# Two blocks of the first projection split into a 4-pair and a 2-pair part, and a new written order of all engines' work

## The chip, the cores and the metric

The kernel runs on one core of a Trainium2 chip. The core has a matrix engine (TensorE, "PE" in the profile, with its weight loads as "PEld"), three engines for element-wise work (VectorE "DVE", ScalarE "ACT", GpSimd "POOL"), and a fifth queue, SyncE ("SP"), which here only issues DMAs. ScalarE and GpSimd issue some DMAs too. Each engine works through its own list in order; semaphores make it wait for the others. The metric is the device time of one execution in microseconds.

## The reference

Attention with normalised queries and keys, then a feed-forward layer. Inputs are `q`, `k`, `v` of 8 batches x 12 heads x 448 positions x 64, gains `g_q`, `g_k`, and the weights `w_in` (768 x 2048) and `w_out` (2048 x 768), all float32.

```python
def rmsnorm(x, g):
    rms = np.sqrt(np.mean(x * x, axis=-1, keepdims=True) + 1e-06)
    return x / rms * g
q_n, k_n = (rmsnorm(q, g_q), rmsnorm(k, g_k))
scores = scale * np.matmul(q_n, k_n.transpose(0, 1, 3, 2))
...
attn = attn / (np.sum(attn, axis=-1, keepdims=True) + 1e-09)
return np.matmul(attn, v).astype(np.float32)
```

The attention's output is laid out as 3584 tokens x 768, and then:

```python
h = x @ w_in
g = h * (1.0 / (1.0 + np.exp(-1.702 * h)))
return (g @ w_out).astype(np.float32)
```

## The kernel before

**Pairs, batches and halves.** Two heads make a pair: 48 pairs, numbered 0 to 47, six to a batch. A pair's 448 positions stand on 112 partitions as four slices. The pairs of batch 0 are worked in two halves of the query positions (half 0, half 1); all later pairs are worked whole. In this text a step is named by its letter and its numbers:

- L(i,w): load of q (w=0), k (1) or v (2) of pair i, 224 KB, a DMA of SP or ACT (`load`, L860).
- S(i): squares, on ACT or POOL (`square`, L869). R(i): their sums, on DVE (`reduce`, L878). In pairs 0 and 1 each of them is split in two.
- Q(i): one over the root. In batch 0 by a logarithm and an exponential on ACT (`by_log`, L892); later for three pairs at once, a seed Q0 on DVE and eight small instructions on POOL.
- N(i,g): q (g=0) or k (1) times that, as bf16, on POOL or DVE (`norm`, L926).
- T(i,g): transpose to 64 x positions, on TensorE for pairs 0 to 11 (four small matmuls), by DMA for later ones. KQ(i), K(i): copies of it out of PSUM, K with the gains; for later pairs KQ scales in place, on DVE or ACT.
- V(i): v as bf16, on DVE or POOL (`vcast`, L933).
- C(i,h,t): scores, on TensorE. E(i,h,t): their exponential, on ACT, 112 x 896 elements. Two PSUM tiles take turns, so a score waits for the exponential two before it.
- P(i,h,w,x): attention times values, on TensorE, into one PSUM tile. O(i,h,w): the division, on DVE, which frees that tile.
- B(i,h): transpose of the result, on TensorE for pairs 0 to 11. X(i,h): its copy into the columns of the first projection's input, `xt`, on DVE.
- F(b,m): a block of the first projection of batch b (`first`, L1221). For batch 0 a block is 12 matmuls of 128 x 224: two slices of the 2048 columns of `w_in`, by six pairs, for one half of the positions; blocks 0 to 7 are half 0. H(b,m): tanh on ACT. G(b,m): the gate on DVE, which frees the block's PSUM bank.
- Y(p,t,h,c): a quarter of a token tile of the second projection of batches 2p and 2p+1. From batch 1 on part of the second projection, and in the last two batches of the first too, is done with seven products in place of eight, with sums of operands made on DVE (TT, S1 to S4, WT, XT).
- WI(c): four DMAs of 768 KB that POOL issues, a quarter of `w_in` each (`load_in`, L1193). Blocks 0 and 1 read WI(0), blocks 2 and 3 WI(1), 4 and 5 WI(2), 6 and 7 WI(3). WO(c): the same for `w_out` (`load_out`, L1199); Y(0,t,0,c) read WO(0) and WO(1), Y(0,t,1,c) WO(2) and WO(3).

**What sets the order.** The order of every engine's list is written out by hand in the table `ORDER` (L206 on), which also says on which engine a step runs that can run on two. A planner in the class `_Order` (L33) walks through these lists when the program is built, with a cost for each step, and emits the instructions in the order of its own clock. This clock decides nothing on an engine's order. It decides three smaller things: which free PSUM bank or output buffer a step takes, how many fill matmuls stand in a planned gap of TensorE (`fill`, L825; they multiply by zeros and write an unused bank), and, in the first 70 us of its clock, a dependency that keeps some POOL instruction behind a DVE instruction which uses the port that both share (`after_lock`, L848). The planner's constants at the top of the file (L25 to L30) tell how DMAs share the bandwidth and how long they take to begin.

**DMA lanes.** The DMAs of SP and ACT take eight semaphores in turn, so the ninth is issued only when the first has landed. A load also waits until its buffer is free: there are seven buffers for rows while i is below 14, so L(7,w) waits for N(0,g), L(13,w) for N(6,g).

**PSUM banks.** Until block F(0,0) two banks serve T and B ("w"); from that block on there are three, and the blocks of the projections take them too. A block holds its bank from its first matmul to its gate.

**The order at the start.** TensorE's list has F(0,0) after C(4,1,1), F(0,1) after B(1,1), and then one block every few steps up to F(0,15); the second projection's Y(0,0,0,0) follows. F(0,0) needs X(0..5, half 0). ACT's list has the squares, the Q steps and the exponentials of batch 0; a table load stands just before E(3,1,1) and H(0,0).

Of the kernel before, what the change touches and what calls it, by code (L numbers as in the profile page):

```python
# [24 lines left out]
BOTH, WITH_SW, SW_WITH = 0.63, 0.52, 0.65  # L25
BEGIN = {"SP": 740.0, "ACT": 760.0, "POOL": 3600.0, "DVE": 1010.0, "PE": 1400.0, "none": 0.0}
LANES, LANDS, KNOWN = 8, 1850.0, 500.0
NEVER = 1e12
APART = 45000.0
# [3 lines left out]
class _Order:  # L33
# [36 lines left out]
    def run(self):  # L70
# [74 lines left out]
        while emitted < len(self.tasks):  # L145
# [40 lines left out]
            if t.moves:  # L186
                t.rest, t.there, t.end = t.moves, free[eng] + LANDS, NEVER
# [14 lines left out]
    def open(self, name, now):  # L202
# [5 lines left out]
        ('R', 0, 1), ('R', 0, 0), ('R', 1, 0), ('R', 1, 1), ('N', 0, 1), 'g', ('KQ', 0), 'gG',  # L208
        ('K', 0), ('R', 2, 0), ('R', 3, 0), ('KQ', 1), ('K', 1), ('N', 2, 0), ('O', 0, 0, 0),
        ('R', 4, 0), ('KQ', 2), ('K', 2), ('KQ', 3), ('V', 1), ('X', 0, 0), ('K', 3), ('V', 2),  # L210
        ('O', 1, 0, 0), ('KQ', 4), ('K', 4), ('R', 5, 0), ('O', 2, 0, 0), ('X', 1, 0), ('V', 5),
        ('O', 3, 0, 0), ('N', 5, 1), ('X', 2, 0), ('KQ', 5), ('K', 5), ('O', 4, 0, 0), ('X', 3,
        0), ('X', 4, 0), ('O', 0, 1, 0), ('R', 6, 0), ('O', 5, 0, 0), ('X', 5, 0), ('X', 0, 1),
        ('O', 1, 1, 0), ('R', 7, 0), ('R', 8, 0), ('Q0', 8), ('X', 1, 1), ('O', 2, 1, 0), ('G',
        0, 0), ('O', 3, 1, 0), ('X', 2, 1), ('G', 0, 1), ('R', 10, 0), ('X', 3, 1), ('O', 4, 1,
        0), ('G', 0, 2), ('KQ', 6), ('K', 6), ('G', 0, 3), ('X', 4, 1), ('O', 5, 1, 0), ('G', 0,
        4), ('R', 9, 0), ('G', 0, 5), ('KQ', 7), ('K', 7), ('G', 0, 6), ('KQ', 8), ('X', 5, 1),
        ('K', 8), ('R', 11, 0), ('Q0', 11), ('G', 0, 7), ('G', 0, 9), ('G', 0, 8), ('V', 6),
        ('N', 11, 1), ('G', 0, 10), ('N', 10, 0), ('N', 10, 1), ('N', 11, 0), ('O', 7, None, 0),
        ('G', 0, 12), ('G', 0, 11), ('G', 0, 13), ('O', 6, None, 0), ('N', 9, 1), ('N', 9, 0),  # L220
        ('G', 0, 14), ('R', 12, 0), ('G', 0, 15), ('R', 13, 0), ('KQ', 9), ('K', 9), ('O', 7,
        None, 1), ('R', 14, 0), ('O', 6, None, 1), ('Q0', 14), ('KQ', 11), ('V', 8), ('KQ', 10),
# [438 lines left out]
def kernel(  # L661
# [22 lines left out]
    HALF = DM // 2  # L684
    WIN = 128
    AW = (NS - 1) * SS + WIN
    ON_PE = NP * 2
    FILL, FILL_GAPS = 1.2, 0.6
    SINGLE = NP

# [131 lines left out]
    def bank():  # L822
        return banks[od.got]
# [977 lines left out]
```

## Time and profile before

| | us |
|---|---|
| median of 5 runs | 412.49 |
| lowest, highest | 412.06, 413.67 |
| the profiled execution, whole | 412.19 |
| its span | 410.4 |
| TensorE busy | 401.7 (98%) |
| VectorE busy | 307.7 (75%) |
| ScalarE busy | 300.9 (73%) |
| GpSimd busy | 179.8 (44%) |

The profile is of one execution. Its span runs from the first instruction to the last; 1.8 us of the execution's own time lie around it. A line of the order-of-time view has the start in us, the length in us, the engine, the source line, the operation, the tiles (out<-in), the shape and the count; what stands in brackets is the idle time of the engine just before and what ended it. A group that follows without a bracket came with no idle time before it. Matmuls are pipelined, so the length of a group of them is longer than the time after which the next can start; the spacing from start to start says what one costs. The granted clock is the share of full speed that TensorE was given: 0.996 on the mean here.

### The profile page before, as it was taken

The page shows a single profiled execution, that of the slowest core. Times are in us where ns is not written, and L with a number is a line of the kernel's source. Part 1 is how long each engine was busy: PE and PEld are TensorE (multiplying, and loading weights), DVE is VectorE, ACT ScalarE, POOL GpSimd, SP SyncE. Part 2 cuts the span into 40 slices and gives each one's busy share as a digit, 9 for nine tenths or more (in the row PEclk, how much of TensorE's full clock was granted, in tenths as well). Part 3 has the DMA queues.
Part 4 walks back from the last instruction along what each step waited for, and adds up shares of the span by engine and source line. Part 5 has one row for each costly group of instructions (what it writes and reads, how often), then busy time and mean ns, then how long its engine had stood idle before and what let it go on. Part 6 is the DMA issues. An engine that isn't in the chain of part 4 may idle for free.

```text
span 410.4 us, 9991 instructions
## 1 busy us (share of the span) xinstructions
PE 401.7 (98%) x3848; PEld 237.6 (58%) x3848; DVE 307.7 (75%) x628; ACT 300.9 (73%) x452; POOL 179.8 (44%) x272
## 2 busy tenths in 40 slices
PE   6999999999999999999999999999999999999996
PEld 5658876565555555565555555555555665555664
DVE  3879897789899977867786687878665889653742
ACT  4899887898887878887897767878888624584211
POOL 5787915974926194839614368346700200000000
PEclk9899999999999999999999999999999999999999
DMA  8999999969584797764875795954653124000065
GB/s 210 239 243 236 239 227 249 233 164 200 150 222 94 184 198 205 189 166 115 222 196 135 150 237 135 182 125 118 169 124 69 43 56 122 2 0 2 14 171 144
DMA packets 101776, 63.38 MB, mean 154 GB/s; under 512 B 55008, under 2 KB 101728, under 8 KB 101728
## 3 DMA queue, kind: packets, MB, share of 16 engines
q1 hardware_dynamic: 91840, 53.98, 54.9%
q0 software_dynamic: 7360, 6.29, 9.5%
q10 hardware_dynamic: 2528, 2.47, 2.5%
q8 instruction: 30, 0.49, 0.5%
q14 instruction: 18, 0.15, 0.1%
HBM read 45.61 MB, written 11.01 MB: 138 GB/s over the span
## 4 chain that ended last, share of the span: by engine, by line
PE 91%; DMA 2%; ACT 2%; POOL 1%; DVE 1%; issue 1%; DVEq 0%; ACTq 0%
PE w L1226 27%; PE w L1321 21%; PE o L1020 13%; PE sc L999 11%; PE b L1321 6%; PE b L1610 4%; PE w L1256 4%; PE w L1610 3%; DMA rows<-in_k_dram 2%; ACT sq L876 1%; ACT att L1009 1%; PE w L952 1%; POOL row L929 1%; PE w L1046 1%; POOL late L942 1%
## 5 line engine op out<-in xcount | busy, mean ns | idle before, releaser
L1007 ACT ACTIVATE att<-sc 112x896 bf16<-112x896 f32 x168 | 146.1, 917 | 26.7 <-PE sc L999 26.3
L1226 PE MATMUL w<-xt,w_in_s 128*128 128x448 bf16 (+1 forms) x672 | 120.9, 326 | 0.1
L1020 PEld LDWEIGHTS <-att 112*128 112x128 bf16 x1536 | 66.6, 98 | 35.7 <-issue 12.3
L1226 PEld LDWEIGHTS <-w_in_s 128*128 128x128 bf16 x672 | 60.5, 97 | 40.6 <-issue 6.5
L929 POOL TENSOR_TENSOR row<-rows,rs 112x512 bf16<-112x512 f32 x66 | 71.3, 1101 | 14.3 <-DMA qk<-row 7.9
L1248 DVE SCALAR_TENSOR_TENSOR g<-th,w 128x448 bf16<-128x448 f32 x96 | 57.5, 615 | 15.1 <-ACT th L1236 15.1
L1020 PE MATMUL o<-vx,att 112*128 112x65 bf16 x1280 | 65.3, 194 | 0.8 <-ACT att L1009 0.6
L1236 ACT ACTIVATE th<-w 128x448 f32<-128x448 f32 x96 | 51.1, 550 | 19.8 <-PE w L1226 16.4
L885 DVE TENSOR_REDUCE ssq<-sq 112x16 f32<-112x1024 f32 (+1 forms) x50 | 58.2, 1168 | 8.1 <-ACT sq L876 7.2
L999 PE MATMUL sc<-qk 64*128 64x448 bf16 (+1 forms) x360 | 47.6, 345 | 0.1
L942 POOL TENSOR_TENSOR vx<-rows,ones 112x512 bf16<-112x512 f32 x21 | 22.3, 1064 | 48.7 <-PE o L1020 43.5
L1031 DVE TENSOR_TENSOR obs<-o,rcp 112x256 bf16<-112x256 f32 x96 | 40.7, 424 | 3.3
L871 POOL TENSOR_TENSOR sq<-rows 112x512 f32<-112x512 f32 x27 | 29.6, 1116 | 23.5 <-DVE ssq L885 9.6
L1030 DVE RECIPROCAL rcp<-o 112x4 f32<-112x4 f32 x96 | 17.1, 178 | 28.8 <-PE o L1020 28.4
L1321 PEld LDWEIGHTS <-late 128*128 128x128 bf16 x304 | 27.4, 97 | 16.9 <-issue 1.1
L876 ACT ACTIVATE sq<-rows 112x1024 f32<-112x1024 f32 (+1 forms) x32 | 32.2, 1017 | 5.9 <-DMA rows<-in_k_dram 4.5
L1321 PEld LDWEIGHTS <-g 128*128 128x128 bf16 x288 | 25.6, 97 | 18.8 <-issue 4.3
L1321 PE MATMUL w<-w_out_s,g 128*128 128x384 bf16 x160 | 31.3, 326 | 0.0
L918 POOL TENSOR_TENSOR t<-rs 112x48 f32<-112x48 f32 x28 | 8.3, 296 | 50.3 <-DVE rs L906 49.2
L1321 PE MATMUL w<-w_out_s,late 128*128 128x384 bf16 x144 | 27.4, 326 | 0.0
L1321 PE MATMUL w<-late 128*128 128x384 bf16 x128 | 24.5, 326 | 0.1
L1009 ACT ACTIVATE att<-sc 112x896 bf16<-112x896 f32 x24 | 20.8, 915 | 0.6 <-PE sc L999 0.5
(135 smaller groups left out, 507.2 us busy)
## 6 DMA issues: line engine op xcount, KB each, us to landing
rows<-in_k_dram SPq DMA_DIRECT2D x42, 224.0 KB, 3.7
rows<-in_q_dram SPq DMA_DIRECT2D x41, 224.0 KB, 3.7
rows<-in_v_dram SPq DMA_DIRECT2D x40, 224.0 KB, 3.4
w_in_s<-in_moe_w_in_dram POOLq DMA_DIRECT2D x4, 768.0 KB, 13.1
w_out_s<-in_moe_w_out_dram POOLq DMA_DIRECT2D x4, 768.0 KB, 19.6
out_dram<-osb SPq DMA_DIRECT2D x10, 168.0 KB, 2.9
out_dram<-osb SPq DMA_DIRECT2D x11, 144.0 KB, 2.6
late<-in_v_dram SPq DMA_DIRECT2D x6, 224.0 KB, 7.7
```

The lines of the kernel that those rows point to most:

```text
L871: made = [nc.gpsimd.tensor_tensor(out=sq[i % N_SQ][:SS, g], in0=raw[turn(i, N_RAW, K_RAW)][:SS, g], in1=raw[turn(i, N_RAW, K_RAW)][:SS, g] ...
L876: nc.scalar.activation(out=sq[i % N_SQ][:SS, part], in_=raw[turn(i, N_RAW, K_RAW)][:SS, part], func=ACT.Square)
L885: nc.vector.reduce_sum(out=ssq_of[g0][:SS, i - g0, part], in_=sq[i % N_SQ][:SS, part], axis=AX.X)
L929: return eng.tensor_tensor(out=row_ring[i % N_QKN][:SS, gi].rearrange("p n (h d) -> p h n d", h=2), in0=raw[turn(i, N_RAW, K_RAW)][:SS, gi ...
L999: nc.tensor.matmul(sc[:, hp, j * SH:j * SH + n], lhsT=qkw[r, k0:k0 + WIN], rhs=qk[r, 0, qs], start=True, stop=True)
L1007: nc.scalar.activation(out=att[:SS, t, :, :S], in_=sc, func=ACT.Exp)
L1020: nc.tensor.matmul(os_[u, w][:, x, :], lhsT=att_of(u)[:SS, kc, hp, qs * SS:qs * SS + WIN], rhs=vx_ring[turn(i, N_V, K_V)][:SS, hp, kc, :], ...
L1031: nc.vector.tensor_tensor(out=to[:SS, :, w, :] if h is None else to[:SS, :2].rearrange("p n h d -> p (n h) d"), in0=o[:SS, :, :D], in1=rcp ...
L1226: nc.tensor.matmul(gps[b, m][:, j * SH:j * SH + n], lhsT=w_in_s[:, ki, f * 128:(f + 1) * 128], rhs=xT[b][:, ki, lo:lo + n], start=(ki == 0 ...
L1236: nc.scalar.activation(out=th[:, :], in_=gps[b, m][:, :S], func=ACT.Tanh, scale=0.851)
L1248: nc.vector.scalar_tensor_tensor(out=g_of[b // 2][:, f:f + len(g), lo:lo + n], in0=view(ths.pop((b, m))[:, :]), scalar=1.0, in1=view(gps.p ...
L1321: nc.tensor.matmul(held[to], lhsT=lhs[:, ko, :], rhs=y[:, ko, :], start=first and ko == 0, stop=ko == NK - 1, skip_group_check=not first)
```

## The change

The first two blocks of the first projection of batch 0 are each made of two steps. F(0,0,0) and F(0,1,0) multiply the columns of pairs 0 to 3; F(0,0) and F(0,1), the same names as before, now multiply those of pairs 4 and 5 only. The four steps are linked in this order. The third bank is opened at F(0,0,0). Since two slices lie side by side in one bank, only the first matmul of a split block starts the bank anew.

The planner is told that the DMAs of POOL take 3700 in place of 1850 to begin, and two of its three bandwidth shares differ by 0.01.

The table `ORDER` is written anew for the whole kernel. In TensorE's list F(0,0,0) stands after B(0,1) and F(0,1,0) after C(2,1,1), F(0,0) after P(1,1,0,1), F(0,1) and F(0,2) after P(1,1,0,3). After the first two batches the list differs by local swaps, and its last 132 steps are the same. The other engines' lists differ more, and 116 steps run on another engine: DVE has 511 steps for 515, ACT 446 for 453, POOL 145 for 134, SP 265 for 265, TensorE 891 for 889. Of the first pairs: L(0,0), L(2,1), L(4,1), L(4,2) move from SP to ACT and L(0,1), L(0,2), L(1,2), L(2,0) from ACT to SP; N(0,1), N(2,0), N(5,1), N(9,g), N(10,g), N(11,g) and V(2) move from DVE to POOL and N(3,g), N(6,0), V(0), V(3), V(4), V(7) from POOL to DVE; S(9), S(11), S(13) move from ACT to POOL.

```diff
-BOTH, WITH_SW, SW_WITH = 0.63, 0.52, 0.65
+BOTH, WITH_SW, SW_WITH = 0.63, 0.53, 0.64
...
-LANES, LANDS, KNOWN = 8, 1850.0, 500.0
+LANES, LANDS, LANDS_SW, KNOWN = 8, 1850.0, 3700.0, 500.0
...
-                t.rest, t.there, t.end = t.moves, free[eng] + LANDS, NEVER
+                t.rest, t.end = t.moves, NEVER
+                t.there = free[eng] + (LANDS_SW if eng == "POOL" else LANDS)
...
+    EARLY = 4
...
+        split = len(kis) < KI
         for j, (f, lo, n) in enumerate(blocks(b, m)):
             for ki in kis:
                 nc.tensor.matmul(gps[b, m][:, j * SH:j * SH + n],
                                  lhsT=w_in_s[:, ki, f * 128:(f + 1) * 128],
-                                 rhs=xT[b][:, ki, lo:lo + n], start=(ki == 0), stop=(ki == KI - 1))
+                                 rhs=xT[b][:, ki, lo:lo + n], start=(ki == 0 and not (j and split)),
+                                 stop=(ki == KI - 1), skip_group_check=split)
...
-               widen=[("w", 3)] if b == m == 0 else None)
+               widen=[("w", 3)] if b == m == kis[0] == 0 else None)
...
+            if b == m == 0:
+                for kis in (range(EARLY), range(EARLY, KI)):
+                    for j in range(2):
+                        project(0, j, kis)
```

The heads of four of the lists of `ORDER`, in the short names used here (L01 is L(0,1)):

```
ACT before:  L01 L10 L20 S0 S0 L31 S1 Q0 L02 L40 L50 Q1 L12 S2 S3 E E Q2 S4 Q3 E E Q4 S5 ...
ACT after:   L00 L10 L31 L21 S0 S0 S1 Q0 L41 L40 L50 S3 Q1 S2 L42 Q3 E Q2 S4 E E E Q4 S5 ...
SP before:   L00 L11 L30 L21 L22 L41 L70 L51 L32 L42 L52 L60 L61 L71 L81 L80 L101 L100 L91 L110 L90 L131 ...
SP after:    L01 L11 L30 L20 L22 L12 L02 L70 L51 L80 L32 L52 L61 L60 L71 L90 L91 L81 L130 L110 L62 L72 ...
DVE before:  R0 R0 R1 R1 N01 g KQ0 gG K0 R2 R3 KQ1 K1 N20 O R4 KQ2 K2 KQ3 V1 X K3 V2 ...
DVE after:   R0 R0 R1 R1 g KQ0 gG R3 K0 R2 N30 N31 KQ1 K1 V0 R4 KQ2 K2 V1 KQ3 K3 O R5 ...
POOL before: S1 N00 N10 N11 V0 WI0 N21 N30 N31 N40 N41 WI1 V3 V4 N50 S6 WI2 S7 S8 WI3 Q8 N60 N61
             N71 N70 N81 N80 WO0 WO1 WO2 V7 WO3 Q11 S14 ...
POOL after:  S1 N00 N01 N11 N10 N20 N21 WI0 V2 N41 N40 WI1 N50 N51 S6 S7 WI2 S8 WI3 Q8 N61
             N70 N71 N80 S9 N81 WO0 WO1 S11 WO2 Q11 N100 N90 N91 N101 N110 S13 N111 V9 WO3 Q14 ...
```

## The prediction

> **What bounds the kernel now.** I read the busy time by stretch first, then the fill matmuls alone, then TensorE, ScalarE and GpSimd in order of time, then the landings of the weights.
>
> Busy time by stretch (length, then PE, PEld, DVE, ACT and POOL busy with instructions, granted clock, DMA share, GB/s):
>
> ```profile
> 0.00:33.20 33.20, 28.72 (x359) 19.19 (x360) 22.44 (x54) 25.29 (x39) 24.83 (x48) 0.95 1.07 232
> 33.20:406.60 373.40, 372.94 (x3492) 218.38 (x3490) 284.87 (x573) 275.61 (x414) 154.96 (x225) 1.00 0.64 148
> 406.60:410.40 3.80, 0.00 (x0) 0.00 (x0) 0.36 (x1) 0.00 (x0) 0.00 (x0) 0.97 0.40 115
> ```
>
> From 33.2 us TensorE is busy for 372.94 of 373.40 us, and no wait of it is listed there. The change adds no matmul to that work, so time can only come out of the first 33.2 us, and any new wait behind it adds to the end. In the first stage the matmuls at L843 do nothing (PE, PEld, clock, DMA, GB/s, of that line alone):
>
> ```profile
> 0.00:33.20 33.20, 13.91 (x87) 8.67 (x87) 0.95 1.07 232
> ```
>
> TensorE by time: fills, the first values product, and the first two blocks of the first projection:
>
> ```profile
> 12.77 1.60 PE L843 MATMUL w<-zeros,ident 128*128 128x240 bf16 x7
> 14.99 0.69 PE L1020 MATMUL o<-vx,att 112*128 112x65 bf16 x16 [0.61 <-ACT att L1009]
> ...
> 33.19 1.32 PE L1226 MATMUL w<-xt,w_in_s 128*128 128x224 bf16 x12
> ...
> 35.56 1.31 PE L1226 MATMUL w<-xt,w_in_s 128*128 128x224 bf16 x12
> ```
>
> ScalarE sets that pace. One square waits 1.59 us for pair 3's keys, and exponentials then run back to back:
>
> ```profile
> 9.62 1.06 ACT L876 ACTIVATE sq<-rows 112x1024 f32<-112x1024 f32 x1 [0.16 <-issue]
> 12.27 1.06 ACT L876 ACTIVATE sq<-rows 112x1024 f32<-112x1024 f32 x1 [1.59 <-DMA rows<-in_k_dram]
> ...
> 27.31 6.96 ACT L1009 ACTIVATE att<-sc 112x896 bf16<-112x896 f32 x8 [0.29 <-PE sc L999]
> 34.29 1.28 ACT L713 ACT_TABLE_LOAD   x1
> ```
>
> GpSimd's issues of the weights:
>
> ```profile
> 14.16 0.92 POOL L1195 DMA_DIRECT2D w_in_s<-in_moe_w_in_dram  x1
> ...
> 45.41 2.73 POOL L1201 DMA_DIRECT2D w_out_s<-in_moe_w_out_dram  x3
> 48.14 1.08 POOL L942 TENSOR_TENSOR vx<-rows,ones 112x512 bf16<-112x512 f32 x1
> 49.12 0.94 POOL L1201 DMA_DIRECT2D w_out_s<-in_moe_w_out_dram  x1
> ```
>
> and the time from issue to landing, w_in_s, then w_out_s:
>
> ```profile
> DMA to landing us min/median/max: 11.1/13.1/14.6
> ```
> ```profile
> DMA to landing us min/median/max: 12.1/19.6/28.1
> ```
>
> Single landings in the trace: the four w_in chunks at 28.71, 34.90, 40.69 and 44.72 us (the first has the 14.6), the four w_out chunks at 57.50, 62.92, 69.99 and 77.18. Row loads of 224 KB land one per 0.95 us from 4.4 us on, in order of issue, eight outstanding at most.
>
> **The yardstick.** For a place in TensorE's list I add up the useful work ahead of it, by start-to-start spacings of the trace: P 0.13, T 0.20, C of half a pair 0.29, C of a whole pair's two steps 0.48, projection block 1.15, B 0.10 or 0.20, Y quarter 0.65. Its start less that sum is what TensorE has lost so far. Before: F(0,0) has 13.1 us ahead and starts at 33.19, lost 20.1; F(0,2) 17.5, 37.75, lost 20.2; F(0,4) 21.5, 41.88, lost 20.3; Y(0,0,1,2), a quarter of the second projection, 55.7, 77.14, lost 21.4. The end moves as this loss moves.
>
> **The early blocks.** F(0,0,0) and F(0,1,0), 8 matmuls of 0.096 us each, stand behind 10.8 and 12.7 us of work, F(0,2) behind 15.4, F(0,4) behind 19.8. Their work is taken out of the two old blocks (12 matmuls become 8+4): nothing added. The built program has 81 fills instead of 87; six at 0.107 us spacing are 0.6 us, and they stand where the walk below already counts time.
>
> **Loads and first squares.** Keys of pair 3 go third on ACT's queue and land with the sixth place, 8.4 us (was 12.2); keys of pair 2 now issue as the ninth at 4.4 and land at 11.25. The three load issues ahead of S(3) sit on ACT, and the last waits for the landing of q2 at 9.36, so S(3) runs 9.75-10.8. Q(1), which ran at 8.91, now stands behind it (10.7-11.25); S(2) 11.3-12.35. VectorE takes R(3) before K(0): 10.85-12.05, so K(0) ends at 12.4 (was 11.13) and C(0) follows; E(0) at 12.9 (was 13.23). Then S(4) waits for q4 at 15.04, idling ACT 0.75 us. Walking on with 0.84 per exponential in a run, 1.04 per square and 0.5 per Q, S(5) ends at 19.95 and E(2) begins at 19.85 (was 19.68). The wait for k3 is gone, but q4's wait and the swapped order take it back: 0 to 0.2 us later.
>
> **GpSimd.** N(0,1) (1.04 there, 0.69-0.89 on VectorE) and N(2,0), N(2,1) stand before the first w_in issue, V(0) no longer. Q(1) at 11.25 puts N(1) at 11.3-13.4; N(2,0) waits for Q(2) at 14.3 and, by the one-port dependency, for N(3,0) and N(3,1), which now run on VectorE until 15.0; so the first weight issue moves from 14.16 to about 17.1, with V(2) and N(4) behind it. The issue-to-landing time is bounded by 11.1 and 14.6; I take 14.6, the same chunk with the same eight loads outstanding: it lands at 31.65. Exponentials and F(0,0,0)'s columns are ready at 29.95. TensorE would stand 1.7 us, with C(3,1,0) queued behind, for which ACT's E(3,1,0) waits (31.2 to 32.6), and so P(5). O(5) stands behind R(6) and R(7) on VectorE, and B(5) and X(5), which the last two pairs' half needs, behind it. F(0,2) then starts at about 36.1, lost 20.7: against 20.2, a loss of 0.5. With 11.1 nothing is waited for, F(0,2) starts at 35.2, lost 19.8: a gain of 0.4; if also O(5) isn't held, a gain of 0.9. Taken +0.4, nearer the row of the same chunk. SP now stops at L(13,0), which waits for N(6) near 40; with 26 loads out instead of 29 the shared traffic ends near 30 us, so chunks 2 to 4 come by 35, 39 and 42, no wait.
>
> The Trainium skill, "DMA: Bandwidth & Descriptors", "Anatomy of one DMA", gives 2.0 us plus bytes over 436e3 for such a transfer: an estimate of 3.8 us for 768 KB. The row has 14.6 under load, so the measurement decides; by the page the chunk would be there at 21 us, and the early blocks would gain the 0.4.
>
> **The rest of the list.** S(9), S(11), S(13) (2.04 each) move from ScalarE and N(9) to N(11) (1.02 each) from VectorE to GpSimd, V(7) leaves it. GpSimd was idle there from 55 to 60 us; that cover is used up. The first w_out issue comes at 46.5, the third behind S(11) at 51. Between third and fourth now stand Q(11) (2.9, seed ready near 55), six N (6.1), S(13) (2.04) and V(9) (1.05): the fourth issue comes at 67.2, was 49.12. The old one was queued behind others. With the first w_out chunk's 3.5 us from issue to first byte its data starts at 70.7. The four chunks' data took 6.7, 4.0, 7.2 and 9.75 us and landed 0.6 to 3.3 us after: 7.2 and 2 give 79.9, the ends 75.3 and 82.5. Y(0,0,1,2), the first reader, has 58.15 us ahead of it and comes at 58.15 + 21.4 + 0.4 = 80.0. Before, it came within 0.1 us of its landing; now again the margin is nothing, with an uncertainty of 2.5 us to both sides, of which only the late side costs. I take +0.5, bounds 0 and +2.5; what waits is all of TensorE behind it. Waits that the clock gate adds are within 0.2: the clock stood at 0.5 from 10.8 to 14.2, while little but fills ran, and the longer gap before C(0) may hold it so for a second 3.4 us. Other swaps are local; from 62 to 90 us VectorE, ScalarE and GpSimd are each 16 to 22% idle, which covers them: 0, bounds -0.1 and +1.0. The planner's new constants put nothing on the chip but the order, the fills and the choice of banks.
>
> Sum: +0.4 +0.5 = +0.9 on the profiled run's 412.19 us (span 410.4 and 1.8 around it), which stands 0.3 under the median of 412.49. On the median: **413.4 us**.
>
> **Rivals.** *Weights in time:* GpSimd's queue serves a late issue faster than the first w_in chunk: that one had 5.4 us to its first byte, the first w_out chunk 3.5, which alone puts the landing at 29.8. The early blocks then start when their columns are there: -0.4 to -0.9, so 411.6 to 412.1, say 411.6. For it: rows of 11.1 and 12.1. Against: those had less traffic beside them. It ends on the other side, and decides from a landing in under 12.9 us (or a first issue before 15.4). *Nothing comes of it:* the early blocks run where the old ones ran, since ScalarE's run of exponentials and the table load (34.29) still set when X(5) is there, and neither weight is missed: within 0.5, 412.7. *Late rows:* SP's stop at L(13,0) leaves k10 and q10 landing near 50.0, where S(10) on ScalarE stands at 50.2 with E(7) behind; another 2 us there is 2 us of TensorE: 415.0. For it: k3's wait shows such a square holding everything; against: margins of other squares were 1 to 6 us.
>
> **Numbers.** Forecast case (412.9 to 414.2) 0.41, weights in time 0.22, nothing 0.20, late rows 0.17. Range 411.4 to 415.6: the full gain with 0.2 more, and both large stalls partly; outside it 0.2. No change is within 0.2% (0.8 us), about what can be told. Faster: 0.22, nearly all of the first rival. Slower: 0.46, late rows and seven tenths of the forecast case. Same: 0.32. The likeliest case's own range is 412.9 to 414.2.
>
> **What would show it.** First w_in issue near 17; a wait of TensorE on L1229's 8 matmuls before 32 us with its release by a DMA; first square of pair 3 near 9.75; a gap ahead of L1260 near 80. Wrong: first w_in issue before 15.4, F(0,2) before 35.5, or TensorE idle anywhere between 45 and 75.

## The result, and the profile after

| | before | changed |
|---|---|---|
| median | 412.23 us (94 executions, 410.0 to 414.16) | 411.3 us (50 executions, 409.51 to 413.43) |
| ratio, 95% interval | | 0.9982, 0.9974 to 0.9989 |
| the profiled execution, whole and span | 412.19, 410.4 | 411.87, 410.1 |

The changed kernel is faster by 0.9 us. I had forecast 413.4; the measured time lies 0.1 us under the low end of the range, on the side of the rival "weights in time". Two later measurements beside before gave 0.9971 (0.995 to 0.9991) and 0.998 (0.9958 to 1.0002). Single executions that ran far slower than the others of their kernel (one of 128 of the kernel before, one of before_fill, three of split_nofill) are left out of all ratios and of the medians below.

Busy time by stretch, changed kernel (length, then PE, PEld, DVE, ACT and POOL busy with instructions, granted clock, DMA share, GB/s), and then the fills at L845 alone:

```profile
0.00:33.20 33.20, 28.94 (x350) 20.02 (x352) 23.46 (x55) 24.87 (x39) 24.37 (x48) 0.95 1.08 230
33.20:406.30 373.10, 372.33 (x3494) 216.86 (x3493) 284.19 (x569) 270.69 (x407) 173.31 (x242) 1.00 0.63 148
406.30:410.10 3.80, 0.00 (x0) 0.00 (x0) 0.36 (x1) 0.00 (x0) 0.00 (x0) 0.78 0.37 112
```
```profile
0.00:33.20 33.20, 12.94 (x81) 8.77 (x81) 0.95 1.08 230
```

Fills went from 13.91 to 12.94 us, and TensorE does 0.22 us more in the first stretch although fills are 0.97 us fewer: more useful work stands there. Behind it TensorE is idle for 0.77 us where it was idle for 0.46.

TensorE by time around the early blocks (start, length, count, and in brackets the idle time before):

```profile
29.92 0.94 PE L1229 MATMUL w<-xt,w_in_s 128*128 128x224 bf16 x8 [0.45 <-DMA w_in_s<-in_moe_w_in_dram]
...
32.01 0.94 PE L1229 MATMUL w<-xt,w_in_s 128*128 128x224 bf16 x8
...
33.74 0.55 PE L1229 MATMUL w<-xt,w_in_s 128*128 128x224 bf16 x4
...
34.39 1.70 PE L1229 MATMUL w<-xt,w_in_s 128*128 128x224 bf16 x16
```

F(0,0,0) and F(0,1,0) stand at 29.92 and 32.01, their second parts at 33.74 and 34.39, and F(0,2) follows inside the last line, at 34.77. The weights are waited for, but for 0.45 us and not for 1.7. By the prediction's yardstick (start less the useful work ahead):

| lost before | before | changed |
|---|---|---|
| F(0,2) | 20.21 | 19.35 |
| F(2,0) | 23.80 | 22.58 |
| F(3,15) | 25.25 | 24.11 |
| F(4,8) | 26.49 | 25.66 |
| F(4,15) | 26.72 | 26.50 |
| F(5,15) | 27.86 | 27.63 |

So the lead is 0.86 us at F(0,2), 1.2 us at F(2,0), 1.1 us at F(3,15), 0.8 us at F(4,8), and 0.2 us from F(4,15) on; the profiled executions end 0.3 us apart, while the medians are 0.9 us apart: the changed kernel's profile is of an execution 0.57 us above its median. In this execution two waits take most of the lead back (TensorE by time):

```profile
240.75 0.30 PE L1022 MATMUL o<-vx,att 112*128 112x65 bf16 x4 [0.22 <-DVE obs L1033]
```
```profile
258.49 0.42 PE L1022 MATMUL o<-vx,att 112*128 112x65 bf16 x8 [0.46 <-DVE obs L1033]
```

By start-to-start spacing they cost 0.38 and 0.62 us; the brackets, 0.22 and 0.46, count from the modelled ends. They are not in every execution: in after_third, a later profile of the same kernel (411.02 us), no wait is listed from 45 us on, and the lead is 1.2 us at F(0,2) and still 1.1 us at F(5,15). The second wait is of a kind that the prediction had put at nothing. VectorE and GpSimd just before it:

```profile
255.17 1.50 DVE L931 TENSOR_TENSOR row<-rows,rs 112x512 bf16<-112x512 f32 x1
256.59 1.21 DVE L887 TENSOR_REDUCE ssq<-sq 112x16 f32<-112x1024 f32 x1
```
```profile
255.08 2.49 POOL L873 TENSOR_TENSOR sq<-rows 112x512 f32<-112x512 f32 x2
```

N(41,1) was moved from GpSimd to VectorE. There it took 1.50 us beside two squares of GpSimd (which took 2.49 in place of 2.04), R(44) follows, and O(34,0) that TensorE needs stands behind both.

ScalarE at the steps of the prediction's walk, and GpSimd's first and last weight issues:

```profile
9.57 1.06 ACT L878 ACTIVATE sq<-rows 112x1024 f32<-112x1024 f32 x1 [2.03 <-DVE gG L1071]
...
14.77 1.06 ACT L878 ACTIVATE sq<-rows 112x1024 f32<-112x1024 f32 x1 [0.62 <-DMA rows<-in_q_dram]
...
31.26 1.78 ACT L1011 ACTIVATE att<-sc 112x896 bf16<-112x896 f32 x2 [0.84 <-PE sc L1001]
33.06 1.28 ACT L715 ACT_TABLE_LOAD   x1
```
```profile
16.68 0.92 POOL L1197 DMA_DIRECT2D w_in_s<-in_moe_w_in_dram  x1
```
```profile
65.85 0.96 POOL L1203 DMA_DIRECT2D w_out_s<-in_moe_w_out_dram  x1
```

and from issue to landing, w_in_s, then w_out_s:

```profile
DMA to landing us min/median/max: 9.3/11.5/13.6
```
```profile
DMA to landing us min/median/max: 9.8/15.0/17.9
```

The first w_in chunk landed at 29.87 (13.2 us after its issue; I had taken 14.6 and 31.65), the last w_out chunk at 75.66 (9.8 us; I had 79.9), 3.5 us ahead of its reader Y(0,0,1,2) at 79.18. The issues themselves were foreseen to 0.4 and 1.4 us.

### The profile page after: what moved, and what is told of

It is laid out like the page before. It is cut to its first block, busy times and chain, and to the rows that moved or that the text cites. A ratio compares the mean times of both kernels' runs of the same rounds, so it can differ in the third digit from the quotient of the medians.

```text
span 410.1 us, 9973 instructions
## 1 busy us (share of the span) xinstructions
PE 401.3 (98%) x3842; PEld 236.9 (58%) x3842; DVE 308.0 (75%) x624; ACT 295.6 (72%) x445; POOL 197.7 (48%) x289
## 4 chain that ended last, share of the span: by engine, by line
PE 89%; DMA 6%; DVE 2%; ACT 0%; issue 0%; SPq 0%; ACTq 0%; DVEq 0%
PE w L1229 26%; PE w L1325 21%; PE o L1022 12%; PE sc L1001 10%; PE b L1325 7%; PE b L1614 5%; PE w L1260 4%; DMA w_in_s<-in_moe_w_in_dram 3%; DMA rows<-in_q_dram 3%; PE w L1614 3%; DVE ssq L887 1%; PE w L954 1%; PE w L1048 1%; DVE obs L1033 0%; DVE g L1252 0%; DVE row L931 0%
## 5 line engine op out<-in xcount | busy, mean ns | idle before, releaser
L931 POOL TENSOR_TENSOR row<-rows,rs 112x512 bf16<-112x512 f32 x70 | 75.0, 1090 | 15.0 <-DMA qk<-row 10.5
L1240 ACT ACTIVATE th<-w 128x448 f32<-128x448 f32 x96 | 50.9, 550 | 19.5 <-PE w L1229 16.0
L873 POOL TENSOR_TENSOR sq<-rows 112x512 f32<-112x512 f32 x37 | 39.5, 1086 | 21.6 <-DMA rows<-in_q_dram 12.8
L1325 PEld LDWEIGHTS <-late 128*128 128x128 bf16 x312 | 28.3, 97 | 19.7 <-issue 2.9
L1032 DVE RECIPROCAL rcp<-o 112x4 f32<-112x4 f32 x96 | 17.1, 178 | 26.1 <-PE o L1022 25.3
L878 ACT ACTIVATE sq<-rows 112x1024 f32<-112x1024 f32 (+1 forms) x27 | 27.2, 1012 | 6.1 <-DMA rows<-in_q_dram 3.9
L1325 PE MATMUL w<-w_out_s,g 128*128 128x384 bf16 x152 | 29.4, 326 | 0.0
L920 POOL TENSOR_TENSOR t<-rs 112x48 f32<-112x48 f32 x28 | 9.2, 328 | 34.7 <-DVE rs L908 29.5
L1325 PE MATMUL w<-late 128*128 128x384 bf16 x136 | 25.7, 326 | 0.0
L1325 PE MATMUL w<-w_out_s,late 128*128 128x384 bf16 x128 | 24.1, 326 | 0.0
```

The lines of the kernel that those rows point to most:

```text
L873: made = [nc.gpsimd.tensor_tensor(out=sq[i % N_SQ][:SS, g], in0=raw[turn(i, N_RAW, K_RAW)][:SS, g], in1=raw[turn(i, N_RAW, K_RAW)][:SS, g] ...
L931: return eng.tensor_tensor(out=row_ring[i % N_QKN][:SS, gi].rearrange("p n (h d) -> p h n d", h=2), in0=raw[turn(i, N_RAW, K_RAW)][:SS, gi ...
L1240: nc.scalar.activation(out=th[:, :], in_=gps[b, m][:, :S], func=ACT.Tanh, scale=0.851)
L1325: nc.tensor.matmul(held[to], lhsT=lhs[:, ko, :], rhs=y[:, ko, :], start=first and ko == 0, stop=ko == NK - 1, skip_group_check=not first)
```

## Experiments

In the recorded expectations "Theory A" is that the early blocks carry the gain, "Theory B" that the new order of loads, squares and exponentials does, and "Theory C" that the waits at 240.2 and 257.7 us give a part of it back. Each block of runs shares the runs of the kernel before on its chip; ratios are to those. A profile is one execution, and may be away from the kernel's median by 2 us; where that matters it is said.

### 1. The parts of the change

**no_split**: the new order without the early blocks.

```diff
-            if b == m == 0:
-                for kis in (range(EARLY), range(EARLY, KI)):
-                    for j in range(2):
-                        project(0, j, kis)
 TensorE's list:  ... B(0,1) [-F(0,0,0)] C(3,1,0) ... C(2,1,1) [-F(0,1,0)] B(5,0) ...
```

> The changed kernel with blocks F(0,0) and F(0,1) whole again, at the places where their last two pairs stood; all else as changed. Theory A (the early blocks carry the gain): TensorE's loss at F(0,2) goes from 19.35 us back to about 20.1, as before the change, and the time is 0.7 us above the changed kernel (412.0 where that has 411.3). Theory B (the new order of loads, squares and exponentials carries it): the loss at F(0,2) stays within 0.2 of 19.35 and the time within 0.2 us of the changed kernel.

**split_only**: the early blocks in the old order, nothing else.

```diff
 TensorE's list before:  ... P(5,0,0,0) B(0,1) [+F(0,0,0)] ... C(2,1,1) B(5,0) [+F(0,1,0)] P(1,1,0,0) ...
```

> The kernel before with the two early steps F(0,0,0) and F(0,1,0) put in after B(0,1) and B(5,0), nothing else moved. Theory A: the loss at F(0,2) falls from 20.2 to 19.6-19.9 (of the 0.6 us lost between P(5) and F(0,0) most is filled), time 0.3 to 0.6 us under before. Theory B: loss and time as before, within 0.2. A third outcome would be a loss above 20.2, because scores and values behind the early steps are held back: time 0.3 above before.

Before 412.68; no_split 412.09, ratio 0.9981 (0.9962 to 1.000); split_only 415.88, ratio 1.0073 (1.0048 to 1.0098). The early blocks alone, with the fills that the planner added for them, cost 3.2 us. (All six executions of split_only had a mean clock under 0.998; against the 17 of 29 of the kernel before that had it too, it is 2.7.) Where it is lost, ScalarE and then TensorE by time in split_only show:

```profile
33.38 1.73 ACT L1010 ACTIVATE att<-sc 112x896 bf16<-112x896 f32 x2 [0.76 <-PE sc L1000]
36.26 0.92 ACT L1010 ACTIVATE att<-sc 112x896 bf16<-112x896 f32 x1 [1.15 <-PE sc L1000]
37.19 1.28 ACT L714 ACT_TABLE_LOAD   x1
```
```profile
39.47 1.08 PE L844 MATMUL w<-zeros,ident 128*128 128x240 bf16 x9 [1.10 <-DVE xt L1051]
40.48 0.36 PE L1000 MATMUL sc<-late 64*128 64x224 bf16 x4
```

In the old order the scores that ScalarE needs next stand behind the early blocks. These two of its waits are for scores, and its run of exponentials ends at 37.2 and not at 34.3; 1.0 us of this was there at 28.3 us already, ahead of the first early block, in an execution whose clock stood at 0.5 from 16.3 to 19.7. TensorE then does nothing useful from 38.2 to 40.48: 1.10 us of waiting for the bank of nine fills, and the fills. (The largest wait of TensorE that this profile lists, 2.01 us for an exponential, ends at 15.05, long before the early blocks, where the kernel before has fills and a wait of 0.61; the expectation of split_nofill below takes it for an effect of theirs.)

In the changed kernel the table load stands at 32.7 to 33.6 us in the profiles that weren't otherwise delayed. This is not ScalarE running ahead: the new list has 18 exponentials before the table load, the old one 20, at 0.84 us each, so with the table load at 33.06 for 34.29 ScalarE is by this count some 0.4 us behind. What the new order does is to put the table load and H(0,0) ahead of exponentials that stood before them. That this is what makes room for the early blocks is likely and was not tested by itself.

**split_nofill.** The planner answers each changed list with other fills: split_only has 95 in place of 87, ten of them behind 36 us. I took those out.

```diff
-        elif now < 45000.0:
+        elif now < 32000.0:
             n = idle * 0.85 / 103
         else:
-            n = (idle - 400.0) * FILL_GAPS / 103 if idle > 900.0 else 0.0
+            n = 0
```

> The kernel before with the two early blocks alone (as in the run of that name, 415.9 us, ratio 1.0073), but without the ten fill matmuls that the program then puts behind 36 us, where its planner expects TensorE to wait. In that run TensorE lost 3.6 us more up to F(0,2) than before. Fills theory: the ten fills (0.107 us each, 1.1 us) and the wait of 1.1 us on their own output bank are cost of the fills, so 1.1 to 2.2 us go: ratio 1.002 to 1.005. Order theory: the wait of 2.0 us of the values product for an exponential is the cause, and fills only stand where TensorE would wait anyway: the time stays within 0.4 us of 415.9, ratio 1.006 to 1.009. If the early blocks by themselves are a gain and the fills took it, the ratio is under 1.000.

414.79, ratio 1.0063 (1.004 to 1.0086), on another chip. The ratio lies in the order theory's range: by the medians two thirds of the cost stay without the fills, by the ratios more. Whether the fills cost nothing or up to 1.1 us (the medians are 3.2 and 2.2 us above those of the kernel before beside them), these intervals do not tell.

**no_split_nofill** and **after_third.** no_split had 92 fills where the changed kernel has 81, eight of them just where the early blocks are missing. Without these eleven, beside the changed kernel itself:

> The changed kernel's order without the early blocks (F(0,0) and F(0,1) whole, where the halves of the last two pairs stood), and without the eleven fill matmuls that the program then adds, so that it has the 81 fills of the changed kernel. Combination theory: the new order lets ScalarE finish its exponentials 1 to 1.7 us earlier, but TensorE then waits ahead of F(0,0), and only the early blocks turn that into useful work: 0.5 to 1.0 us slower than the changed kernel beside it, ratio to before 0.999 to 1.001, lost time at F(0,2) 20.3 to 20.8. Order theory: the order alone brings the gain and the eleven fills hid it: within 0.3 us of the changed kernel, lost time 19.3 to 19.8.

> The changed kernel as it is, beside the next three on their chip. Two measurements gave 0.9982 and 0.9971; expected 0.997 to 0.9985, table load of ScalarE between 32.7 and 33.6 us (before: 34.3), lost time at F(0,2) 19.0 to 20.0.

Before 412.94; changed kernel 411.81, ratio 0.998 (0.9958 to 1.0002); no_split_nofill 411.69, ratio 0.9988 (0.9969 to 1.0007). The medians do not tell the two apart, so the combination theory's 0.5 to 1.0 us for the early blocks was not seen, and the intervals do not exclude it either. The two profiles of the order without early blocks are of executions 1.3 and 2.3 us above their kernel's median; they show where the blocks are missing. TensorE by time in no_split:

```profile
31.48 0.99 PE L845 MATMUL w<-zeros,ident 128*128 128x240 bf16 x8
...
33.59 1.31 PE L1229 MATMUL w<-xt,w_in_s 128*128 128x224 bf16 x12
```

Eight fills stand where the changed kernel has its second early block. F(0,2) has lost 20.7 us there and 21.9 in no_split_nofill, whose clock stood at 0.5 from 32.7 to 36.1. Which share of the gain is the order's is taken up under experiment 5.

### 2. The two late waits

**two_back**: N(41,1) back on GpSimd, and O(32,1) ahead of X3(1,5) on VectorE. **norm_back**: the first of these alone. **late_before**: the changed kernel's lists for all that its planner starts in the first 204 us, the lists of before for the rest.

```diff
 GpSimd's list:   ... N(41,0) [+N(41,1)] ...
 VectorE's list:  ... [-N(41,1)] ...      two_back also:  [+O(32,1)] X3(1,5) U(1,6,1) [-O(32,1)]
```

> The changed kernel with two local moves undone: N(41,1) on GpSimd again, after N(41,0), and O(32,1) ahead of X3(1,5) on VectorE. In the changed kernel's trace TensorE waits 0.38 us at 240.2 and 0.62 us at 257.7 for VectorE's O. Theory C (these two waits give part of the gain back): both waits gone, TensorE's end 1.0 us earlier than the changed kernel's 406.25, ratio to before 0.996 to 0.997. Rival: the waits only move to another place or the slower step on GpSimd makes a new one; end within 0.3 us of 406.25.

> The changed kernel's order for what its plan starts in the first 204 us, and for the rest the order of the kernel before. Theory C: the 1.2 us by which the changed kernel leads at F(3,15) (lost 24.1 against 25.25) stays to the end: end of TensorE near 405.4, ratio to before 0.997. Rival (the lead is lost wherever the later work waits for its weights or sums, whatever the order): end near 406.2, ratio as the changed kernel's 0.998.

> The changed kernel with N(41,1) back on GpSimd behind N(41,0), nothing else. This takes out the second of the two late waits, 0.62 us at 257.7. Wait theory: the loss from 240 to 262 us shrinks by 0.6 us, the time by 0.5 to 0.7 us, ratio 0.9950 to 0.9965. Slack theory: something just behind (a slot of the weights, the scores of the next batch) was as late, and the wait only moves, as the first wait did when O(32,1) was moved: within 0.2 us of the changed kernel, ratio 0.9965 to 0.998.

two_back 411.66, ratio 0.9971 (0.9954 to 0.9988); late_before 411.34, 0.9967 (0.9948 to 0.9986); norm_back 411.37, 0.9968 (0.9951 to 0.9985). All three are faster than before; none is told apart from the changed kernel. In norm_back's trace the second wait is gone; GpSimd and TensorE at the same place:

```profile
254.71 2.05 POOL L931 TENSOR_TENSOR row<-rows,rs 112x512 bf16<-112x512 f32 x2
256.71 2.04 POOL L873 TENSOR_TENSOR sq<-rows 112x512 f32<-112x512 f32 x2
```
```profile
257.51 0.42 PE L1022 MATMUL o<-vx,att 112*128 112x65 bf16 x8
```

There is no bracket: TensorE did not wait. One such pair of profiles would not show it, since after_third lists no wait there either; all the profiles do. From F(4,8) to F(4,15) it took 11.4 us in all three with N(41,1) on GpSimd and otherwise the same late order (norm_back, two_back, wi_late_norm). With N(41,1) on VectorE it took 12.0 in seven profiles of ten, 11.6 in two and 11.4 in one. The first wait is another matter. In two_back it came back under another name:

```profile
241.09 0.81 PE L1325 MATMUL w<-late,g 128*128 128x384 bf16 x4 [0.63 <-DVE osb L1355]
```

VectorE has O(32,1) and two steps for an output tile (`osb`) due at about the same time there; the changed kernel waits for O, which stands last, and two_back for an `osb` step. For the second wait Theory C is shown in the traces, up to 0.6 us and not in every execution; in the medians 0.6 us is at the edge of what these runs can tell, and it wasn't seen.

### 3. The landing of the first w_in chunk

**wi_early** issues it before N(2,0), **wi_late** behind N(4,0); **after_again** is the changed kernel beside them.

```diff
 GpSimd's list, wi_early:  ... N(1,0) [+WI(0)] N(2,0) N(2,1) [-WI(0)] V(2) N(4,1) N(4,0) WI(1) ...
 GpSimd's list, wi_late:   ... N(1,0) N(2,0) N(2,1) [-WI(0)] V(2) N(4,1) N(4,0) [+WI(0)] WI(1) ...
```

> The changed kernel as it is, again beside the kernel before, so that the next three have it on their own chip. The first measurement gave 0.9982. If the two waits at 240.2 and 257.7 us are in every execution and single executions of the first 42 us differ by 0.6 us and more, as three profiles of the same early order suggest (lost time at F(0,2) 19.35, 19.93 and 19.74 us), the ratio is again 0.997 to 0.999, and the lost time at F(0,2) lies between 19.3 and 20.0. If the first ratio was a chance of one chip, it is 1.000 or above.

> The changed kernel with its first w_in issue moved ahead of N(2,0) and N(2,1) on GpSimd, that is from 16.7 us to about 13.3 to 14.2, where GpSimd stood idle for 1.5 us. Weights theory (the landing of the first chunk, not the exponentials, releases the early blocks): the chunk lands near 27 us, the wait of 0.45 to 1.0 us ahead of F(0,0,0) goes, and the time falls by 0.3 to 0.8 us against the changed kernel, ratio 0.996 to 0.997. Pace theory (ScalarE's run of exponentials and the table load set when P(5) and F(0,2) come, so earlier weights only lengthen another wait): F(0,0,0) may move up, but F(0,2) stays at 34.8 to 35.3 and the time is that of the changed kernel within 0.2 us. If the earlier chunk takes bandwidth from the row loads of pairs 3 to 6, a square of ScalarE waits longer and the time rises by up to 1 us.

> The changed kernel with its first w_in issue moved behind V(2) and N(4) on GpSimd, from 16.7 us to about 19.9, directly ahead of the second. This measures what a late first chunk costs, the term that the prediction took at +0.5 net. Weights theory: with the 13.2 us from issue to landing of the changed kernel it lands near 33.1, F(0,0,0) waits 3 us more, and F(0,2) loses 2 to 3 us: ratio 1.003 to 1.006. With 11.1 us, the fastest of the four before, it lands at 31.0 and costs 0.5 to 1.0 us. Pace theory (TensorE has 1 us or more to spare until P(5) in any case): F(0,0,0) waits, but F(0,2) is under 1 us later.

Before 412.3; changed kernel 411.07; wi_early 413.47, ratio 1.0023 (0.9997 to 1.0048); wi_late 412.25, ratio 0.9997 (0.9974 to 1.0019). Against the changed kernel beside it wi_early is 2.4 us slower; wi_late is 1.2 us slower, which is near the edge of what twelve executions tell, and each also has more fills than the changed kernel's 81 (90 and 95). The landings of the chunk:

| kernel | issue | landing |
|---|---|---|
| wi_early | 13.35 | 27.06 |
| changed, three profiles | 16.60, 16.68, 16.81 | 28.76, 29.87, 30.03 |
| wi_late | 20.06 | 29.64 |

An issue 3.4 us later did not land later. In wi_late the first 26 row loads had all landed by 26.2, and the chunk came 3.5 us behind them; in the changed kernel these rows came until 30.9 to 32.0, in turn with the chunk. By the chunk's packets in the two traces (16.68 and 20.06) the first byte came 5.1 and 3.5 us after the issue, the data took 6.4 and 4.5 us, and the landing followed 1.7 and 1.5 us behind. The DMA engines move 244 and 251 GB/s from 8 to 28 us, and what lands when is a matter of what else is in the queues. wi_early shows the other side of it. GpSimd, VectorE and TensorE in wi_early:

```profile
13.35 0.92 POOL L1197 DMA_DIRECT2D w_in_s<-in_moe_w_in_dram  x1
...
28.63 2.04 POOL L873 TENSOR_TENSOR sq<-late 112x512 f32<-112x512 f32 x2 [3.82 <-DVE xt L1052]
```
```profile
30.70 1.22 DVE L887 TENSOR_REDUCE ssq<-sq 112x16 f32<-112x1024 f32 x1 [1.24 <-POOL sq L873]
32.69 1.22 DVE L887 TENSOR_REDUCE ssq<-sq 112x16 f32<-112x1024 f32 x1 [0.78 <-POOL sq L873]
...
34.22 0.42 DVE L1033 TENSOR_TENSOR obs<-o,rcp 112x256 bf16<-112x256 f32 x1
```
```profile
34.70 0.27 PE L1048 MATMUL w<-ident,obs 112*128 112x112 bf16 x2 [1.95 <-DVE obs L1033]
```

The chunk came 2.8 us earlier than in the first profile of the changed kernel, and the wait of F(0,0,0) was gone. But the q rows of pair 6 landed at 28.49 instead of 23.96 (after_again), GpSimd stood 3.8 us for them (the releaser that the line names had long been done; the landing is 0.14 us before the start), the sums R(6) and R(7) on VectorE followed late, and O(5) behind them held TensorE for 1.95 us at B(5,0). This is the chain that the prediction had feared of a late chunk; it came of an early one. (F(0,2) follows at 38.09 in this profile; a stretch at a clock of 0.5 from 34.9 to 38.3 is part of that.)

**wi_late_nofill, wi_late_norm.** wi_late has eight fills ahead of F(0,0,0) where the changed kernel has two. The first of these two runs leaves them out, the second also has N(41,1) back on GpSimd.

```diff
-        elif now < 45000.0:
+        elif now < 28500.0:
```

> The changed kernel with the first w_in issue behind V(2) and N(4) on GpSimd (16.7 to 20 us), without the eight fill matmuls that the program then puts ahead of F(0,0,0). With those it took 412.25 us beside 411.07 of the changed kernel, and its chunk, issued at 20.06, landed at 29.64. Traffic theory (the landing is set by what the shared DMA engines have to move ahead of it, so 3.4 us in the issue are not 3.4 us in the landing): the chunk lands at 29 to 30.5 again, the row loads behind it land earlier, and the time is that of the changed kernel within 0.4 us, ratio 0.996 to 0.998. Issue theory (13.2 us from issue to landing, the single profile was an exception): it lands near 33, F(0,0,0) waits 3 us, ratio 1.002 or more.

> The kernel of wi_late_nofill with N(41,1) back on GpSimd as well, as a version that may beat the changed kernel. By the profiles the two terms are 0 to 0.4 us (rows of pairs 6 and 7 earlier) and 0.6 us (the wait at 257.7): 0.3 to 1.0 us under the changed kernel, ratio 0.9945 to 0.9965. If late waits only move, as with O(32,1), and the issue theory holds, it is slower than the changed kernel by 1 us or more.

wi_late_nofill 413.47, ratio 1.0007 (0.9975 to 1.0038); wi_late_norm 411.7, ratio 0.9989 (0.9957 to 1.0021). The landings are those of the traffic theory again: issued at 19.97 and 21.61, landed at 29.79 and 30.44. The times are not. Of the 24 executions those at 0.998 and more end between 409.3 and 411.9, the others between 411.5 and 415.4. That the landing doesn't follow the issue is shown; that a late issue is free is not. The scatter goes with the clock: with the eight fills none of wi_late's 12 executions had a mean clock under 0.998, without them 8 and 6 of 12 had; these are two chips, though, and why the lowered executions of these two kernels are so much longer stays open.

### 4. The landing of the last w_out chunk

**wo_late** moves the fourth w_out issue behind Q(14); **wo_late_nofill** does the same without the 15 fills that the planner then sets ahead of the reader.

```diff
 GpSimd's list:  ... N(11,1) V(9) [-WO(3)] Q(14) [+WO(3)] N(12,0) ...
 wo_late_nofill also:
-            n = (idle - 400.0) * FILL_GAPS / 103 if idle > 900.0 else 0.0
+            n = 0
```

> The changed kernel with its fourth w_out issue moved behind Q(14) on GpSimd, from 65.9 to about 71.1 us. This tests the sum's other term: the prediction had the fourth chunk landing at 79.9 for a reader at 80.0; in the profile it came 9.8 us after its issue, at 75.7, for a reader at 79.2. If a chunk issued there always takes 9.8 us, it lands near 80.9 and TensorE waits 1.7 us ahead of L1262, which the end keeps: ratio about 1.002. If it takes the 14 us that the prediction took for the same spot (first byte 3.5, data 7.2, 2 and 1 more), it lands at 84 and costs 4 to 5 us, ratio 1.009. If the queue is faster late, below 8.1 us, nothing is seen.

> The changed kernel with its fourth w_out issue behind Q(14), as in the run of that name (414.9 us, 3.8 more than the changed kernel beside it), without the 15 fill matmuls that the program then put ahead of L1262. In that profile the chunk was issued at 73.0 and landed at 80.5, 0.9 us before the reader's place at 81.4; what stood there were the 15 fills (1.6 us) and a wait of 1.03 us for their bank. Fills theory: most of the 3.8 us is the fills', and with 7.5 us from issue to landing the late issue itself costs 0 to 1.0 us: ratio 0.997 to 1.000. Landing theory: the chunk takes the 9.8 us of the changed kernel, lands at 80.8 against a reader at 79.2 to 79.5, and TensorE waits 1.3 to 1.6 us: ratio 1.000 to 1.002, with a wait of L1262's matmuls on the DMA.

wo_late 414.86, ratio 1.0071 (1.0044 to 1.0097); wo_late_nofill 411.88, ratio 0.9975 (0.9956 to 0.9994), which is the changed kernel's. TensorE by time in wo_late:

```profile
82.39 1.70 PE L845 MATMUL w<-zeros,ident 128*128 128x240 bf16 x15 [1.03 <-DVE xt L1052]
83.92 1.30 PE L1260 MATMUL w<-w_out_s,g 128*128 128x384 bf16 x7
```

The chunk was there at 80.48, and yet TensorE did 15 fills and waited 1.03 us for the bank that the fills were to write. Without the fills the chunk, issued at 70.92, landed at 78.21 after 7.3 us, and nothing waited. So the term that the prediction priced at +0.5, with an end of +2.5, has 5 us of issue time to spare; it is the planner's fills for it that cost: from F(0,15) to F(1,0) wo_late lost 3.77 us and the changed kernel 1.06, so 2.7 of the 3.8 us between the medians. The other 1.1 are not explained; that profile also waited 1.57 us for the first w_in chunk, and its clock stood at 0.5 from 31.1 to 34.5.

### 5. The granted clock

Each execution has a mean granted clock, and for the kernel before these fall in two groups. Over the executions whose clock was recorded one by one (for before, those beside the experiments):

```
                         executions   clock under 0.998   median of those   median of the others
before                        127            74                413.05              411.75
changed                        75            20                411.81              411.20
new order, no early blocks     24             7                412.77              411.67
```

In most profiles the lowered clock before the end is a stretch of 0.5, of 3.4 us: from 10.8 to 14.2 in the kernel before, from 12.4 to 15.9 in the changed kernel, 6.8 us long (10.9 to 17.7) in after_again, and in four others one lies later, between 16 and 38 us; seven profiles have none. The Trainium skill, "TensorE: Matmul & The Clock Gate", "Part 1: The HAM clock gate", says that the gate looks at TensorE's activity in a free-running window of about 3.4 us, so that it depends on chance where a kernel falls in it. The lengths of 3.4 and 6.8 us in these traces agree, and that one program has executions with and without such a stretch fits it.

**before_fill** puts six more fills between 8 and 14 us into the kernel before.

```diff
-            n = idle * FILL / 200
+            n = idle * (FILL if idle > 5000.0 else 1.8) / 200
```

> The kernel before with denser fill matmuls between 8 and 14 us (six more; 90% of the planned idle time in place of 60%), nothing else. So far 31 of 58 executions of before show a mean granted clock under 0.998, with a median of 413.0 us against 411.7 of the other 27; of the changed kernel it is 15 of 63. Clock theory: a part of the measured gain is that the changed order leaves TensorE's clock alone more often. Then more fills do it for the kernel before too: under 3 in 10 executions below 0.998, and a median 0.4 to 0.8 us lower, ratio 0.998 to 0.999. Work theory: the share below 0.998 stays near one half and the fills only push steps back by 0.1 us each: ratio 1.000 to 1.002.

412.79, ratio 1.0005 (0.9986 to 1.0023). The share under 0.998 fell, to 2 of 11 from 21 of 34 on that chip; the time did not. The nine others had a median of 412.6, against 411.6 for the others of the kernel before on that chip: the six fills seem to cost as much as the clock gave. So six more fills here went with fewer lowered executions; that this shortens the time was not shown by this run.

By the table the gain has two parts: executions at 0.998 and more differ by 0.55 us between before and changed, and the changed kernel has fewer of the others (27% against 58%; at the 0.6 to 1.3 us by which the groups differ in the two kernels that is 0.2 to 0.4 us). The order without early blocks has the second part (29%) and hardly the first (411.67 against 411.75 and 411.20). That is the best reading I have of which part does what, but the groups were made after the fact and across chips, and the direct comparison on one chip did not separate the two kernels.

## Why the prediction was wrong

**The yardstick and the bound were right.** The time came out of the first 33 us, and the end moved as the loss did: 0.2 us less lost at F(5,15) in the profiled execution, 411.87 for 412.19, and 1.1 us less in after_third, 411.02.

**The step that failed first** is the early blocks' "+0.4": "I take 14.6, the same chunk with the same eight loads outstanding: it lands at 31.65". It landed at 29.87, TensorE stood 0.45 us and not 1.7, and F(0,2) came at 34.77, not at 36.1. In place of a loss of 0.5 there was a gain of 0.86 against the one execution of before; over eight profiles with this early order the loss at F(0,2) ran from 18.98 to 21.37, median 19.5, 0.7 less than 20.21. Of the 1.8 us by which the chunk was early, 0.4 are the earlier issue and 1.4 the shorter time from issue to landing (13.2). The size was off because the step's form was: I added a time from issue to landing to a later issue. With the DMA engines full, a chunk issued 3.4 us later landed at the same time, and one issued 3.3 us earlier came 2.8 us earlier and cost another load its place. The sharing could be read before: "one per 0.95 us from 4.4 us on" holds only to 20.8 us in that trace; from there, beside the chunk's data, the rows landed 1.5 to 2.3 us apart. The rival "weights in time" named the outcome and its time, 411.6: it decided from a landing in under 12.9 us of an issue at 17.1, that is by 30.0, and the chunk landed at 29.87. Its reason was luck: it had 3.5 us to the first byte, which was 5.1, so the 13.2 us are over its 12.9, and the landing was in time because the issue was earlier and the data took 6.4 us for 7.2. Nor did the early blocks start when their columns were there, but 0.45 us later. I had it at 0.22, because I read the bounds 11.1 and 14.6 as properties of a chunk and leaned on the "same" one.

**The w_out term** failed in the same way: "+0.5" from a landing at 79.9, with the data time and the tail of other chunks. The fourth chunk landed 4.2 us sooner: it was issued 1.35 us earlier, its first byte came after 3.4 us as foreseen, its data took 6.0 us for 7.2, and the landing followed 0.35 us behind for 2. The term measured 0, and even 5.1 us of later issue did not use up the margin.

**What was priced at nothing.** "Other swaps are local ... 0, bounds -0.1 and +1.0" covered only 62 to 90 us. A wait of 0.3 us of the kernel before at 132 went, and two came at 240 and 258; in the profiled execution they are worth +1.0 together and stand at the upper bound, in after_third little of it is there. I had looked for idle time of the engines, and had not walked the moved N(41,1) to the O behind it. Its price was there too: the "0.69-0.89" of such a step on VectorE is that of the first pairs; beside GpSimd's steps the kernel before has others of 0.93 to 1.53 us (the longest at 129.7). The clock was put "within 0.2"; its share in the executions halved, which by the table is worth 0.2 to 0.4.

**Step by step:** S(3) at 9.57 (forecast 9.75), S(4)'s wait for q4 0.62 (0.75), E(2) at 19.67 (19.85), first w_in issue at 16.68 (17.1) and fourth w_out issue at 65.85 (67.2) were right. So was the place of the wait, on the first early block and released by the DMA. The gap near 80 did not come, and "F(0,2) before 35.5", named as what would make the forecast wrong, did. "Late rows" and "nothing" did not happen: TensorE has no listed wait between 45 and 240 us.

## What to carry to other kernels

Where the DMA engines are full, do not add a latency to an issue: ask what else is in the queues then (the same chunk's data took 6.4 us beside row loads, and 4.5 us where these ended early). Counting the bytes that are queued ahead and dividing by the rate is the estimate that this suggests; no forecast here was made that way. Moving one transfer up moved another one down, so name the one that loses its place. Before putting steps early on the busy engine, look for the work behind them that feeds the next engine: the same two blocks cost 2 to 3 us in one order and nothing that could be measured in another. That they gain there was not shown. When a list is rewritten, walk every step that changed its engine to the first step behind it that the bounding engine waits for, to the end of the kernel.

## What the runs showed that I had not expected

- The transfers' order is elastic: the first w_in chunk took 13.7, 13.2, 9.6 and 8.8 us from issue to landing at issues of 13.35, 16.68, 20.06 and 21.61. With no row load landing between them the chunks came 3.8 to 3.9 us apart (wi_late: 29.64, 33.42, 37.28, 41.22), some 205 GB/s. The prediction's estimate of 3.8 us by the Trainium skill's "DMA: Bandwidth & Descriptors", "Anatomy of one DMA", is for one transfer from start to end; no such chunk here landed that soon after its issue, the soonest after 7.3 us.
- A step on VectorE beside squares of GpSimd: N(41,1) took 1.50 us, and the two squares 2.49 for 2.04. An N on VectorE with no step of GpSimd beside it took 0.68; with one it took from 0.68 to 1.53. N(41,1) itself took 1.12 in after_third, where TensorE lists no wait for it.
- Executions of the same program differ by 3 us at a clock of 0.998 and more (409.2 to 412.7 for after_third), the loss at F(0,2) by 0.6 us in three profiles; a single profile does not tell a gain of 0.2% from none.
- Fills that the planner sets for a wait that does not come are not free: 15 of them and the wait for their bank cost 2.7 us in wo_late.
